# Attention over channels, then a gated feed-forward layer: q and k loaded eight rows at a time, and the first batch's norms by columns instead of by a row

## The chip, the core and the metric

The kernel runs on one core of one Trainium2 chip. The metric is the device time of one execution in microseconds (us). The engines are named as in the profile: PE (TensorE, matrix products), PEld (its weight loads), DVE (VectorE), ACT (ScalarE), POOL (GpSimd) and SP (SyncE). "DMA" is the 16 engines that move data between the main memory (HBM) and the core.

## The reference

There are four batches of q, k and v, each 6016 x 256, and weights of 256 x 1536 (gate and value) and 1536 x 256 (out). Attention runs between channels, not between tokens:

```python
qn = q / (np.linalg.norm(q, axis=1, keepdims=True) + 1e-06)   # norms over the tokens
kn = k / (np.linalg.norm(k, axis=1, keepdims=True) + 1e-06)
s = kn.transpose(0, 2, 1) @ qn / tau                           # 256 x 256 for each batch
a = np.exp(s - s.max(-1, keepdims=True))
a /= a.sum(-1, keepdims=True) + 1e-09
x = v @ a
gate = 1 / (1 + np.exp(-(x @ w_gate)))
out = (gate * (x @ w_val)) @ w_out
```

Inputs and output are float32; tau is 1.0 and known when the kernel is built.

## The kernel before

**Tiling.** A batch is read as 128 partitions x 47 rows of 256 channels; row t of a partition is one token. Rows go in chunks of four (TPC), twelve chunks to a batch, the last with three rows. DMAs from POOL's queue convert float32 to bf16 on the way. For each row the raw scores q^T k are added up in PSUM (`score`, two products of 128x256, tile ps_s), and the squares of q and k are added up for the norms. The scores are scaled by the inverse norms and exponentiated to e, of 256 x 256 in two halves.

**Folding.** Since x = v a, the kernel never forms x. It computes G = a w_gate and H = a w_val once for each batch (`gh`, 12 products of 2 matmuls each, in three groups of 512 columns, tiles ps_gh, gh_G, gh_H), with the division by the row sums (`sums`) at their eviction. Then, for each chunk of v, transposed (`transpose_v`, for the first two chunks on PE, later by DMA), `glu` makes for each of 12 blocks f the products ps_gate and ps_val (2 matmuls of 128x512 each), the sigmoid on ACT (g_sb) and the product on DVE (hT). `out_mms` multiplies hT by w_out for the chunk before (ps_o), and `flush` copies and stores.

**Order.** The order on every engine is written out by hand. All matmuls go through one helper, so they share the line L89 in the profile and are told apart by their tiles. While batch b is in the feed-forward loop, `side_work(b)` hangs loads, scores and norms of batch b + 1 onto the slots (chunk, f) of that loop. Only the first batch's attention has nothing to hide behind: it is written out ahead of the loop, and it is what the change is about.

**The first batch.** The first chunk of q and k comes over the SP and ACT queues in float32 and is converted by DVE and ACT. All others come over POOL's queue (`load_qk`, L98): ten pairs of transfers of four rows, then two rows and one row. Then follow, on the same queue, the first groups of w_gate and w_val (L144), the first chunk of v (L107), the other two groups of each, v's second chunk and w_out (L151). POOL's transfers share eight semaphores in turn, so each issue waits until the eighth transfer before it has landed. For each chunk DVE squares q and ACT squares k (L183, L181), DVE adds both to acc (L493), and PE makes the scores, followed by products that nobody reads (`busy`, tile ps_busy, five after each chunk), which keep it occupied while it waits for data. The last chunks' squares, and acc, are summed over partitions on PE into ps_n: for q as columns (`norm_q`, one column a product), for k as a row that stands in every partition (`norm_k`, 128x256 products).

**The tail ahead of the loop.** `roots` takes x^(1/2) as exp(ln(x)/2) on ACT (L301, L302), in two parts (q's columns with half of k's row, then the other half); both functions are in the same table as the exponential that follows. `weights` adds the epsilon and inverts on DVE (L273, L274, in `wide_inv`), scales the scores by q's and k's inverse norm in one DVE instruction for each half (L310), and exponentiates (L319). Eight `busy` products stand between. Then come the sums of e (L157, L158 invert them), four `gh` products, v's transposes between them (L400, evicted at L404 and L405), and two more `gh` products; ACT loads the Sigmoid table and the loop begins. Evictions of `gh` are at L383 (ACT) and L385 (DVE). The remaining six `gh` products stand in the loop's first slots:

```python
    gh(0, 4, pso, "o", act=False)
    gh(0, 5, pso, "o", act=False)
    ...
                if (b, ci) == (0, 0) and 0 < f <= len(gh_order) - 6:
                    gh(0, 5 + f, pso, "o")
```

Of the kernel before, what the change touches and what calls it, by code (L numbers as in the profile page):

```python
# [10 lines left out]
FP32 = mybir.dt.float32  # L11
BF16 = mybir.dt.bfloat16
ACT = mybir.ActivationFunctionType
# [5 lines left out]
def kernel(  # L19
# [47 lines left out]
    def pool(name, bufs, **kw):  # L67
        return ctx.enter_context(tc.tile_pool(name=name, bufs=bufs, **kw))

    consts = pool("consts", 1)  # L70
    qkpool = pool("qkpool", NCH)
    sqpool = pool("sqpool", 2)
# [20 lines left out]

    def load_qk(b, t0, nt):
        tiles = []
        for name, src in (("q", q), ("k", k)):
            tl = qkpool.tile([P, TPC, C], BF16, tag=name, name=name + "_sb")
            nc.gpsimd.dma_start(out=tl[:, :nt, :], in_=rows(src, b)[:, t0 : t0 + nt, :])  # L98
            tiles.append(tl)
        qk[b, t0] = tiles  # L100

# [9 lines left out]
    t0, nt = groups0[0]  # L111
    qk[0, 0] = [qkpool.tile([P, TPC, C], BF16, tag=n, name=n + "_sb") for n in ("q", "k")]
    first_f32 = [consts.tile([P, nt, C], FP32, name=f"first{w}") for w in range(2)]
    for eng, tl, src in zip((nc.sync, nc.scalar), first_f32, (q, k)):
        eng.dma_start(out=tl, in_=rows(src, 0)[:, t0 : t0 + nt, :])

    nc.scalar.add_instruction(
        mybir.InstLoadActFuncSet(
            name=nc.get_next_instruction_name(),
            engine=mybir.EngineType.Activation,  # L120
            act_func_set_id=list(get_activation_tables("trn2")).index("natural_log_exp_and_others"),
        )
    )
    load_qk(0, *groups0[1])

    ident_bf = consts.tile([P, P], BF16)
    make_identity(nc, ident_bf)
    ones_bf = consts.tile([P, P], BF16)
    nc.vector.memset(ones_bf, 1.0)
# [6 lines left out]
    nc.scalar.copy(qk[0, 0][1], first_f32[1])  # L136
    for t0, nt in groups0[2:]:
        load_qk(0, t0, nt)

    w_sb = [[consts.tile([P, CB, FG], BF16, name=f"w_{n}{fg}") for fg in range(NFG)] for n in ("gate", "val")]  # L140
    w_out_sb = consts.tile([P, FC, C], BF16)
    for fg in range(NFG):
        for w, src in enumerate((moe_w_gate, moe_w_val)):
            nc.gpsimd.dma_start(  # L144
                out=w_sb[w][fg],
                in_=src.rearrange("(t p) f -> p t f", p=P)[:, :, ds(fg * FG, FG)],
            )
        if fg == 0:
            load_v(0, 0)
    load_v(0, 1)  # L150
# [36 lines left out]

    def norm_q(ps, sq, nt, first, last):

        for u in range(nt):  # L190
            for j in range(CB):
                mm(
                    ps[:, j : j + 1],
                    sq[:, u, ds(j * P, P)],
                    ones_bf[:, 0:1],
                    start=(first and u == 0 and j == 0),
                    stop=(last and u == nt - 1),
                    skip_group_check=True,
                )

    def norm_k(ps, sq, nt, last, parts=1):

        n = C // parts
        for u in range(nt):
            for i in range(parts):
                mm(
                    ps[:, CB + i * n : CB + (i + 1) * n],
                    ones_bf,
                    sq[:, u, ds(i * n, n)],
                    start=False,  # L210
                    stop=(last and u == nt - 1),
                    skip_group_check=True,
                )

# [40 lines left out]
    def norms_mm(b):  # L255

        s = st[b]
        fold_q, fold_k = s["fold"]
        ps = psm.tile([P, CB + C], FP32, tag="m", name="ps_n")
        norm_q(ps, fold_q, 2, True, True)  # L260
        norm_k(ps, fold_k, 2, True)
        s["n"] = ps
# [29 lines left out]

    def roots(b, part):

        s = st[b]
        if part == 0:
            s["n_sb"] = attp.tile([P, CB + C], FP32, tag="nsb", name="n_sb")
            s["r"], s["rk"] = s["n_sb"][:, :CB], s["n_sb"][:, CB:]
        cols = slice(0 if part == 0 else CB + P, CB + (part + 1) * P)
        x = s["n_sb"][:, cols]  # L300
        nc.scalar.activation(out=x, in_=s["n"][:, cols], func=ACT.Ln)  # L301
        nc.scalar.activation(out=x, in_=x, func=ACT.Exp, scale=0.5)  # L302

    def weights(b, i):

        s = st[b]
        wide_inv(b, i)
        y = attp.tile([P, CB, P], FP32, tag=f"y{i}", name="y_sb")
        for j in range(CB):
            nc.vector.scalar_tensor_tensor(  # L310
                out=y[:, j, :],
                in0=s["s"][:, j, ds(i * P, P)],
                scalar=s["r"][:, j : j + 1],
                in1=s["rk"][:, ds(i * P, P)],
                op0=ALU.mult,
                op1=ALU.mult,
            )
        e = attp.tile([P, CB, P], BF16, tag=f"e{i}", name=f"e_sb{i}", bufs=2)
        nc.scalar.activation(out=e, in_=y, func=ACT.Exp, bias=shift)  # L319
        s.setdefault("e", []).append(e)  # L320
        s.setdefault("rrow", [])
# [42 lines left out]

    gh_order = [(0, w, i) for i in range(CB) for w in range(2)]
    gh_order += [(fg, w, i) for fg in range(1, NFG) for w in range(2) for i in range(CB)]

# [21 lines left out]

    def transpose_v(b, ci, ps=None):  # L390

        t0, nt = groups[ci]
        v_sb = vs.pop((b, ci))
        vT = vtpool.tile([P, TPC * CB, P], BF16, tag="vT", name="vT")
        flat = v_sb[:, :nt, :].rearrange("p t c -> p (t c)")
        if ps is None:
            nc.sync.dma_start_transpose(out=vT[:, : nt * CB, :], in_=flat)
        else:
            for n in range(nt * CB):
                nc.tensor.transpose(  # L400
                    out=ps[:, n, :], in_=flat[:, ds(n * P, P)], identity=ident_bf
                )
            half = nt * CB // 2
            nc.scalar.copy(vT[:, half : nt * CB, :], ps[:, half : nt * CB, :])  # L404
            nc.vector.tensor_copy(out=vT[:, :half, :], in_=ps[:, :half, :])  # L405
        vts[b, ci] = vT.rearrange("p (u cb) n -> p cb u n", cb=CB)

# [73 lines left out]
    busy(9)  # L481
    ps_n0 = psm.tile([P, CB + C], FP32, tag="m", name="ps_n")

# [4 lines left out]
    for g, (t0, nt) in enumerate(groups0):  # L488
        engines = (nc.vector, nc.scalar) if g < last0 else (nc.scalar, nc.vector)
        sq = [squares(0, t0, nt, w, engines[w], acc[w] if g == 0 else None) for w in range(2)]  # L490
        if 0 < g < n_acc:
            for w in range(2):
                nc.vector.tensor_tensor(out=acc[w], in0=acc[w], in1=sq[w], op=ALU.add)  # L493
        for u in range(nt):
            score(0, t0, u)
        if g < n_acc:
            busy(5)
        elif g == n_acc:
            norm_q(ps_n0, acc[0], TPC, True, False)
            norm_k(ps_n0, acc[1], TPC, False)  # L500
            norm_q(ps_n0, sq[0], nt, False, False)
            norm_k(ps_n0, sq[1], nt, False)
        elif nt == TPC:
            busy(2)
            norm_q(ps_n0, sq[0], nt, False, False)
            norm_k(ps_n0, sq[1], nt, False)
        elif g < last0:
            held = (sq, nt)
        else:
            (held_q, held_k), n = held  # L510
            norm_q(ps_n0, held_q, n, False, False)
            norm_k(ps_n0, held_k, n, False)
            norm_q(ps_n0, sq[0], nt, False, True)
            norm_k(ps_n0, sq[1], nt, True, CB)
    st[0]["n"] = ps_n0
    for i in range(CB):
        roots(0, i)
    busy(8)
    for i in range(CB):
        weights(0, i)  # L520
    gh_tiles(0)
    sums(0, 0)
    gh(0, 0, psg, "g", act=False)
    gh(0, 1, psv, "v", act=True)
    transpose_v(0, 0, psv.tile([P, TPC * CB, P], BF16, tag="v", name="ps_tp"))
    sums(0, 1, pss, "s")
# [3 lines left out]
    gh(0, 4, pso, "o", act=False)  # L530
    gh(0, 5, pso, "o", act=False)


    def side_work(b):
# [7 lines left out]
        for ci in range(NCH):  # L542
            nb, nci = (b, ci + 1) if ci + 1 < NCH else (b + 1, 0)
            lb, lci = (b, ci + 2) if ci + 2 < NCH else (b + 1, ci + 2 - NCH)
            if (nb, nci) == (0, 1):
                at(8, lambda: transpose_v(0, 1, psm.tile([P, TPC * CB, P], BF16, tag="m", name="ps_tp")))
            elif nb < B:
                at(ci * FC + 2, transpose_v, nb, nci)
# [6 lines left out]
        for g, (t0, nt) in enumerate(groups):  # L555
            s0 = first + g * (last - first) // NCH
            at(max(0, s0 - 20), load_qk, n, t0, nt)
            for u in range(nt):
# [25 lines left out]
    for b in range(B):  # L584
        side = side_work(b)
        for ci in range(NCH):
            block = b + 1 < B and ci in (9, 10)
            for f in range(FC):
# [4 lines left out]
                for fn, a in side.get((ci, f), ()):  # L593
                    fn(*a)
                if (b, ci) == (0, 0) and 0 < f <= len(gh_order) - 6:
                    gh(0, 5 + f, pso, "o")
# [46 lines left out]
```

## Time and profile before

| What | Value |
|---|---|
| median of 3 runs | 833.22 us (833.01 to 833.39) |
| profiled execution | 833.39 us, of which 831.3 us are the span of the profile |
| PE busy | 818.4 us, 98% of the span |
| DVE, ACT, POOL busy | 591.0, 390.6, 82.6 us |
| POOL's transfers (q0) | 38.81 MB written, 23920 packets |
| first gate product | at 43.38 us |
| PE idle before the first sums | 2.03 us, to 38.53 us |

The span is from the first to the last instruction of one execution. A time in the chain or the timeline counts from its start. In a row of the timeline the bracket says how long the engine had stood idle and what ended it. PE's busy time is modelled from the starts of its pipelined matmuls, so 98% busy says that it seldom waits, not that it computes at its peak. GB/s count bytes as they are written, so a load of float32 into bf16 reads twice that.

### The profile page before, as it was taken

What the parts mean: (1) busy time and instruction counts of PE and PEld (TensorE: products, weight loads), DVE (VectorE), ACT (ScalarE), POOL (GpSimd) and SP (SyncE); (2) the same over time, 40 slices, a digit from 0 to 9 for tenths busy, and PEclk for the clock granted to TensorE, in tenths of its full rate; (3) what the DMA queues carried; (4) which work ended last, traced back from release to release, by engine and by line L of the source; (5) the groups of instructions that cost most, each with busy time, mean ns of one, the idle gap of its engine ahead of it and who ended that gap; (6) DMA issues with size and microseconds to landing.
All of it is one profiled execution on the core that took longest, in us unless ns stands there. A gap on an engine that the chain in (4) does not pass through costs nothing.

```text
span 831.3 us, 13764 instructions
## 1 busy us (share of the span) xinstructions
PE 818.4 (98%) x5191; PEld 503.9 (61%) x5204; DVE 591.0 (71%) x1023; ACT 390.6 (47%) x644; POOL 82.6 (10%) x157
## 2 busy tenths in 40 slices
PE   7799999999999999999999999999999999999998
PEld 4546666666665666665566666666566566666666
DVE  6577787787667777778757777777766666666665
ACT  4464444446644444444654444444555444444442
POOL 5531100002111100000221010000000000000000
PEclk9999999999999999999999999999999999999999
DMA  9999522335947423322975353223322423322211
GB/s 210 206 206 208 108 52 54 83 64 109 173 84 133 95 58 84 61 52 60 180 140 103 85 118 64 51 48 89 64 48 61 86 52 79 74 49 65 50 35 71
DMA packets 79026, 77.17 MB, mean 93 GB/s; under 512 B 50800, under 2 KB 55920, under 8 KB 78960
## 3 DMA queue, kind: packets, MB, share of 16 engines
q0 software_dynamic: 23920, 38.81, 27.9%
q1 hardware_dynamic: 54752, 36.91, 17.5%
q8 instruction: 40, 0.66, 0.3%
q10 hardware_dynamic: 288, 0.59, 0.2%
q14 instruction: 26, 0.21, 0.1%
HBM read 78.64 MB, written 24.64 MB: 124 GB/s over the span
## 4 chain that ended last, share of the span: by engine, by line
PE 95%; DMA 3%; DVE 1%; issue 0%; ACT 0%; POOL 0%; DVEq 0%; POOLq 0%
PE ps_o L89 29%; PE ps_gate L89 29%; PE ps_val L89 29%; PE ps_s L89 4%; DMA k_sb<-in_k_dram 3%; PE ps_gh L89 3%; DVE hT L430 0%; PE ps_n L89 0%; DVE sq L183 0%; PE ps_end L89 0%; ACT g_sb L429 0%; PE ps_tp L400 0%; DVE n_sb L274 0%; POOL q_sb L98 0%; DVE n_sb L273 0%
## 5 line engine op out<-in xcount | busy, mean ns | idle before, releaser
L430 DVE TENSOR_TENSOR hT<-ps_val,g_sb 128x512 bf16<-128x512 f32 (+1 forms) x576 | 390.9, 679 | 205.1 <-ACT g_sb L429 199.9
L429 ACT ACTIVATE g_sb<-ps_gate 128x512 bf16<-128x512 f32 (+1 forms) x576 | 338.3, 588 | 385.9 <-PE ps_gate L89 379.1
L89 PE MATMUL ps_val<-vT,gh_H 128*128 128x512 bf16 (+1 forms) x1152 | 337.6, 375 | 0.3
L89 PE MATMUL ps_gate<-vT,gh_G 128*128 128x512 bf16 (+1 forms) x1152 | 337.5, 375 | 0.2
L89 PE MATMUL ps_o<-w_out_sb,hT 128*128 128x256 bf16 x2244 | 324.8, 273 | 0.0
L89 PEld LDWEIGHTS <-hT 128*128 128x128 bf16 x2268 | 221.0, 98 | 124.6
L89 PEld LDWEIGHTS <-gh_H 128*128 128x128 bf16 x1152 | 112.7, 98 | 131.7 <-issue 0.8
L89 PEld LDWEIGHTS <-gh_G 128*128 128x128 bf16 x1152 | 112.5, 98 | 37.4
L107 POOL DMA_DIRECT2D v_sb<-in_v_dram x48 | 25.5, 531 | 622.8 <-DMA vT<-v_sb 513.4
L456 DVE COPY out_sb<-ps_o 128x256 f32<-128x256 f32 x187 | 77.2, 413 | 12.6 <-PE ps_o L89 12.6
L89 PE MATMUL ps_s<-k_sb,q_sb 128*128 128x256 bf16 x376 | 66.0, 272 | 4.9 <-DMA k_sb<-in_k_dram 3.7
L89 PEld LDWEIGHTS <-q_sb 128*128 128x128 bf16 x376 | 36.7, 98 | 13.7 <-issue 6.3
L234 DVE TENSOR_TENSOR acc<-acc,sq 128x1024 bf16<-128x1024 bf16 (+1 forms) x66 | 44.1, 669 | 0.0
L183 DVE TENSOR_TENSOR sq<-q_sb 128x1024 bf16<-128x1024 bf16 (+2 forms) x44 | 29.3, 667 | 2.6 <-DMA q_sb<-in_q_dram 2.6
L98 POOL DMA_DIRECT2D k_sb<-in_k_dram x48 | 26.4, 550 | 17.7 <-DMA k_sb<-in_k_dram 7.9
L98 POOL DMA_DIRECT2D q_sb<-in_q_dram x48 | 26.2, 546 | 15.3 <-DMA q_sb<-in_q_dram 7.2
L183 DVE TENSOR_TENSOR sq<-k_sb 128x1024 bf16<-128x1024 bf16 (+2 forms) x34 | 22.4, 658 | 1.0 <-PE ps_n L89 1.0
L89 PE MATMUL ps_busy<-ones_wide,ones_bf 128*128 128x512 bf16 x61 | 17.3, 416 | 1.7 <-DVE shift L133 1.6
L181 ACT ACTIVATE sq<-k_sb 128x1024 bf16<-128x1024 bf16 (+1 forms) x11 | 11.2, 1018 | 14.5 <-DMA k_sb<-in_k_dram 11.7
L493 DVE TENSOR_TENSOR acc<-acc,sq 128x1024 bf16<-128x1024 bf16 x16 | 11.1, 691 | 5.5 <-ACT sq L181 5.3
L89 PEld LDWEIGHTS <-e_sb 128*128 128x128 bf16 x112 | 10.4, 101 | 7.6 <-ACT e_sb L319 2.7
L89 PE MATMUL ps_gh<-w_val,e_sb 128*128 128x512 bf16 x45 | 14.1, 390 | 0.4 <-issue 0.2
(61 smaller groups left out, 136.6 us busy)
## 6 DMA issues: line engine op xcount, KB each, us to landing
out_dram<-out_sb SPq DMA_DIRECT2D x44, 512.0 KB, 2.9
v_sb<-in_v_dram POOLq DMA_DIRECT2D x44, 256.0 KB, 3.8
q_sb<-in_q_dram POOLq DMA_DIRECT2D x43, 256.0 KB, 7.5
k_sb<-in_k_dram POOLq DMA_DIRECT2D x43, 256.0 KB, 8.6
out_dram<-out_sb SPq DMA_DIRECT2D x3, 384.0 KB, 2.5
w_gate<-in_moe_w_gate_dram POOLq DMA_DIRECT2D x3, 256.0 KB, 6.8
w_val<-in_moe_w_val_dram POOLq DMA_DIRECT2D x3, 256.0 KB, 7.4
w_out_sb<-in_moe_w_out_dram POOLq DMA_DIRECT2D x1, 768.0 KB, 12.6
```

What stands on the lines that cost most here:

```text
L89: nc.tensor.matmul(out, lhsT=lhsT, rhs=rhs, start=start, stop=stop, **kw)
L98: nc.gpsimd.dma_start(out=tl[:, :nt, :], in_=rows(src, b)[:, t0 : t0 + nt, :])
L107: nc.gpsimd.dma_start(out=v_sb[:, :nt, :], in_=rows(v, b)[:, t0 : t0 + nt, :])
L181: nc.scalar.activation(out=sq[:, :nt, :], in_=src[:, :nt, :], func=ACT.Square)
L183: engine.tensor_tensor(out=sq[:, :nt, :], in0=src[:, :nt, :], in1=src[:, :nt, :], op=ALU.mult)
L234: nc.vector.tensor_tensor(out=acc[:, :nt, :], in0=acc[:, :nt, :], in1=st[b]["sq", w][:, :nt, :], op=ALU.add)
L429: nc.scalar.activation(out=g_sb[:, :n], in_=ps_gate[:, :n], func=ACT.Sigmoid)
L430: nc.vector.tensor_tensor(out=hts[b, ci][:, f, :n], in0=ps_val[:, :n], in1=g_sb[:, :n], op=ALU.mult)
L456: nc.vector.tensor_copy(out=out_sb[:, s, :], in_=ps)
L493: nc.vector.tensor_tensor(out=acc[w], in0=acc[w], in1=sq[w], op=ALU.add)
```

## The change

- `load_qk` loads up to eight rows into a tile of eight rows, and gives its halves to the two chunks. The pool has 8 such tiles for q and for k instead of 12 of four rows. For the first batch that is four pairs of eight rows, then 4, 4, 2 and 1; for each later batch six pairs instead of twelve.
- On POOL's queue v's first chunk comes ahead of all weights. POOL also builds an identity in float32.
- The fillers become six after each chunk up to the last pair, one and two in that pair.
- All norms of the first batch, k's too, are summed as columns (ps_n is 128x4), rooted on ACT with Sqrt, and inverted on DVE. ACT then loads the table for Exp. k's inverse norms are spread into a row in every partition by a float32 product with the identity, one for each half (`spread_k`).
- DVE copies the scores to SBUF (`copy_s`), multiplies by the spread row (four times 128x128), and ACT exponentiates four times 128x128 with q's inverse norm as scale.
- Three fillers and one stand around the spreads instead of eight. v's transposes come ahead of the sums. Five instead of six `gh` products stand ahead of the loop, seven in it, and in the second and third group each half's G and H follow one another.

```diff
-    qkpool = pool("qkpool", NCH)
+    qkpool = pool("qkpool", 8)
...
-            tl = qkpool.tile([P, TPC, C], BF16, tag=name, name=name + "_sb")
+            tl = qkpool.tile([P, 2 * TPC, C], BF16, tag=name, name=name + "_sb")
             nc.gpsimd.dma_start(out=tl[:, :nt, :], in_=rows(src, b)[:, t0 : t0 + nt, :])
             tiles.append(tl)
-        qk[b, t0] = tiles
+        for u in range(0, nt, TPC):
+            qk[b, t0 + u] = [tl[:, u : u + TPC, :] for tl in tiles]
...
+    nc.scalar.preload_act_table(ACT.Sqrt)
+    pairs = [(t, 2 * TPC) for t in range(TPC, head - 3 * TPC, 2 * TPC)]
+    loads0 = pairs + [(t, n) for t, n in groups0 if t >= pairs[-1][0] + 2 * TPC]
+    load_qk(0, *loads0[0])
...
-    for t0, nt in groups0[2:]:
+    for t0, nt in loads0[1:]:
         load_qk(0, t0, nt)
+    load_v(0, 0)
...
-        if fg == 0:
-            load_v(0, 0)
...
+    def norms_sqrt(b):
+        s = st[b]
+        s["r"] = attp.tile([P, 2 * CB], FP32, tag="r", name="r")
+        nc.scalar.activation(out=s["r"], in_=s["n"], func=ACT.Sqrt)
+
+    def norms_inv(b):
+        r = st[b]["r"]
+        nc.vector.tensor_scalar(out=r, in0=r, scalar1=1e-6, scalar2=None, op0=ALU.add)
+        nc.vector.reciprocal(r, r)
...
+    def spread_k(b, i, pl, tag):
+
+        s = st[b]
+        ps = pl.tile([P, P], FP32, tag=tag, name="ps_rk")
+        mm(ps, s["r"][:, CB + i : CB + i + 1].to_broadcast([P, P]), ident_f, True, True)
+        s.setdefault("rk", []).append(ps)
...
+        nc.vector.tensor_copy(out=s["x"][:, j, :], in_=s["s"][:, j, :])
...
-        wide_inv(b, i)
-        y = attp.tile([P, CB, P], FP32, tag=f"y{i}", name="y_sb")
+        e = attp.tile([P, CB, P], BF16, tag=f"e{i}", name=f"e_sb{i}", bufs=2)
         for j in range(CB):
-            nc.vector.scalar_tensor_tensor(
-                out=y[:, j, :],
-                in0=s["s"][:, j, ds(i * P, P)],
-                scalar=s["r"][:, j : j + 1],
-                in1=s["rk"][:, ds(i * P, P)],
-                op0=ALU.mult,
-                op1=ALU.mult,
-            )
...
-        nc.scalar.activation(out=e, in_=y, func=ACT.Exp, bias=shift)
+            y = attp.tile([P, P], FP32, tag=f"y{i}{j}", name="y_sb")
+            nc.vector.tensor_tensor(
+                out=y, in0=s["x"][:, j, ds(i * P, P)], in1=s["rk"][i], op=ALU.mult
+            )
+            nc.scalar.activation(
+                out=e[:, j, :], in_=y, func=ACT.Exp, bias=shift, scale=s["r"][:, j : j + 1]
+            )
...
-    gh_order = [(0, w, i) for i in range(CB) for w in range(2)]
-    gh_order += [(fg, w, i) for fg in range(1, NFG) for w in range(2) for i in range(CB)]
+    gh_order = [(fg, w, i) for fg in range(NFG) for i in range(CB) for w in range(2)]
...
-            busy(5)
+            busy(6 if t0 < pairs[-1][0] else 1 if t0 == pairs[-1][0] else 2)
...
     st[0]["n"] = ps_n0
-    for i in range(CB):
-        roots(0, i)
-    busy(8)
-    for i in range(CB):
-        weights(0, i)
+    norms_sqrt(0)
+    nc.scalar.preload_act_table(ACT.Exp)
+    copy_s(0, 0)
+    norms_inv(0)
+    copy_s(0, 1)
+    busy(3)
+    spread_k(0, 0, pso, "o")
+    spread_k(0, 1, pso, "o")
+    busy(1)
+    weights(0, 0)
+    weights(0, 1)
+    late = []
+    transpose_v(
+        0, 0, psv.tile([P, TPC * CB, P], BF16, tag="v", name="ps_tp"), lambda *a: late.append(a)
+    )
+    nc.scalar.copy(*late.pop())
     gh_tiles(0)
     sums(0, 0)
     gh(0, 0, psg, "g", act=False)
     gh(0, 1, psv, "v", act=True)
-    transpose_v(0, 0, psv.tile([P, TPC * CB, P], BF16, tag="v", name="ps_tp"))
     sums(0, 1, pss, "s")
     gh(0, 2, psg, "g", act=False)
     gh(0, 3, psv, "v", act=True)
     nc.scalar.preload_act_table(ACT.Sigmoid)
     gh(0, 4, pso, "o", act=False)
-    gh(0, 5, pso, "o", act=False)
...
-                at(8, lambda: transpose_v(0, 1, psm.tile([P, TPC * CB, P], BF16, tag="m", name="ps_tp")))
+                at(7, lambda: transpose_v(0, 1, psm.tile([P, TPC * CB, P], BF16, tag="m", name="ps_tp")))
...
-            at(max(0, s0 - 20), load_qk, n, t0, nt)
+            if g % 2 == 0:
+                at(max(0, s0 - 20), load_qk, n, t0, min(2 * TPC, NT - t0))
...
-                if (b, ci) == (0, 0) and 0 < f <= len(gh_order) - 6:
+                if (b, ci) == (0, 0) and f < len(gh_order) - 5:
                     gh(0, 5 + f, pso, "o")
```

## The prediction

> **What bounds the kernel now.** I read the page first (engine shares, chain), then the chain of waits in order of time, then one-microsecond windows for the granted clock, and last the timeline of the first 45 us.
>
> ```profile
> span 831.3 us, 13764 instructions
> PE 95%; DMA 3%; DVE 1%; issue 0%; ACT 0%; POOL 0%; DVEq 0%; POOLq 0%
> ```
>
> TensorE (PE) ends 95% of the chain. The windows from 43.4 us to 800 us show it busy all the time but for some 0.05 us in a few stretches. Whatever removes idle time elsewhere than on PE is worth nothing there. What is left is the head: everything ahead of the first gate product. In the chain of waits (start, length, what) it reads:
>
> ```profile
> 20.88 10.61 DMA k_sb<-in_k_dram
> 31.53 1.03 PE ps_s L89 x8
> 34.29 0.49 PE ps_n L89 x10
> 34.81 0.29 ACT n_sb L301
> 35.12 0.32 ACT n_sb L302
> 35.46 0.76 DVE n_sb L273
> 36.24 0.98 DVE n_sb L274
> 37.32 0.62 DVE y_sb L310 x2
> 37.97 0.52 ACT e_sb L319
> 38.53 0.20 PE ps_r L89 x2
> 39.62 0.76 PE ps_tp L400 x8
> 41.17 2.37 PE ps_gh L89 x6
> 43.54 0.43 PE ps_gate L89 x2
> ```
>
> Up to 33.5 us the loads of q and k decide. Then 3.7 us go from the last norm product to the first weights e (34.78 to 38.53), and 4.9 us more to the first gate product: 43.38 us in the timeline. Columns of the next view are stretch, its length, busy us of PE, PEld, DVE, ACT, POOL, then the granted clock, DMA share and GB/s:
>
> ```profile
> 37.00:38.00 1.00, 0.00 (x0) 0.00 (x0) 0.89 (x4) 0.04 (x1) 0.12 (x1) 1.00 1.24 205
> 39.00:40.00 1.00, 1.00 (x10) 0.74 (x9) 0.89 (x5) 0.27 (x1) 0.53 (x1) 0.80 1.23 202
> 41.00:42.00 1.00, 0.82 (x2) 0.30 (x2) 0.65 (x3) 0.29 (x1) 0.30 (x1) 0.50 1.15 213
> 43.00:44.00 1.00, 1.00 (x6) 0.43 (x5) 0.87 (x2) 1.00 (x1) 0.51 (x1) 1.00 1.46 195
> ```
>
> PE stood idle for 2.03 us (36.5 to 38.53), and from about 39.6 to 43.0 us its clock was halved: there a 128x512 product takes 0.42 us instead of 0.215. So the old tail pays twice for its long wait. The weights and v come in the order of the POOL queue, and an issue waits for the eighth before it, so the issues tell the landings:
>
> ```profile
> 18.43 0.53 POOL L98 DMA_DIRECT2D k_sb<-in_k_dram  x1 [0.74 <-DMA k_sb<-in_k_dram]
> 19.66 0.53 POOL L98 DMA_DIRECT2D q_sb<-in_q_dram  x1 [0.70 <-DMA q_sb<-in_q_dram]
> 37.88 0.53 POOL L98 DMA_DIRECT2D q_sb<-in_q_dram  x1 [0.95 <-DMA v_sb<-in_v_dram]
> 39.12 0.53 POOL L98 DMA_DIRECT2D k_sb<-in_k_dram  x1 [0.70 <-DMA w_gate<-in_moe_w_gate_dram]
> ```
>
> One four-row transfer (524 KB read) lands each 1.23 to 1.25 us: 419 to 426 GB/s read, the queue always full. First gate weights landed by 35.1 us, first value weights by 36.37, v's first chunk at 37.88, second gate weights at 39.12.
>
> **The change, part by part.**
>
> *Loads.* 24 issues for the first batch become 16: four pairs of eight rows, then 4, 4, 2, 1. Bytes and their order on the path are the same, and the last transfers are as small as before, so the last k lands at the same 33.4 us if the rate holds. The trace has no eight-row transfer. Nearest rows: the four-row steps of 1.25 us in the middle and 1.5 us around 25 us. As bounds I take 1.23 and 1.35 us for each half of a new transfer; with 16 halves (about 20 us) that is -0.3 to +1.6 us. I take 0, the row nearest. [...] POOL builds one more identity (its two steps took 0.23 and 0.29 us for bf16) before its third issue, while 2 MB are queued: nothing.
>
> *Squares and adds.* They now start in pairs. DVE's three steps per chunk (0.69 each) need 2.07 of the 2.5 us in which a chunk lands. After the last pair (k at 26.55 us as now) DVE finishes at about 26.55 + 1.1 (ACT's square) + 4 x 0.69 = 30.4 us, then squares chunks 9 (31.05) and 10 (31.7). PE's norm products of chunk 9 end at about 31.75, so chunk 10's scores start 0.2 us later than today's 31.53. The 128x256 k-norm products (0.11 each) become twice as many of one column (about 0.045): 0.36 for 0.43 us a chunk. Together the last norm product ends at 34.9 us instead of 34.78. Bounds 34.4 (all caught up) and 35.3.
>
> *Norms to e.* ACT's root is 128x4: nearest row Ln 128x130, 0.28 us; I take 0.25 with hand-over (35.15). Then Exp's table: table loads in this trace take 1.28 us (36.45). Beside it DVE adds and inverts 128x4: 0.15 + 0.17 as for 128x1 (rows L157, L158) up to 0.74 + 0.97 as for 128x130; I take 0.35 (35.5). The two fp32 spreading products are not in the trace: from 0.076 us (a transpose: 8 in 0.61) to about 0.7; I take 0.4 each (36.35). Two scalings at 0.31 each after the first spread end at 36.55; two exponentials of 128x128, at 0.3 each (between 0.28 and 0.51), at 37.1 us. e's first half is there 1.4 us earlier than 38.5. Both copies of the scores (0.41, as L456) lie beside the root and the spreads.
>
> *PE afterwards.* Three fillers, the spreads, a filler and v's eight transposes (0.61; v now comes first and lands near 35.1) fill the wait to 37.2 us, so I expect no halved clock. Sums to 37.35, first gh product (0.43) to 37.8. The second needs the value weights, which are now third in the queue and land near 37.85: this wait is new but short. It ends at 38.3; second sums, products three to five to 39.7. DVE: half of vT 0.42 (37.7), reciprocal 0.35, eviction 0.75 (38.8), reciprocal 0.35, eviction 0.75: 39.9. First gate product at 39.95 us, 3.4 us before today's 43.38. ACT's second value eviction is done at 40.2, ahead of the value product at 40.4; the Sigmoid table (1.28) then ends at 41.5, ahead of the third gate product at 42.4.
>
> *Given back.* Five gh products stand ahead of the loop instead of six; the sixth costs 2 x 0.215 = 0.43 us inside it, where PE has no gap. The order of gh products after the first four changes nothing in count, and their weights (40.4 to 42.9 us) land before use.
>
> *Later batches.* Six pairs of transfers instead of twelve; today's are issued at 199 us for products after 239 us, and PE waits for none after 60 us. Eight tiles of eight rows hold more than twelve of four. For batch 1 the first two transfers (2 MB) should land near 54 us, ahead of the first score at about 57.8. If that cover went, it would cost what they are late: nothing at these numbers.
>
> Sum: -3.43 + 0.43 = -3.0 us. The profiled execution took 833.39 us (831.3 of span, 2.1 around it), the highest of the runs shown, 0.17 above their median of 833.22. So 830.4.
>
> **The rivals.**
>
> *The clock falls elsewhere.* With only one and two fillers in the last pair, and one-column products for norms, the stretch from 29.4 to 32.8 us has about 1.6 us of wide products. For it: 36.2 to 39.6 us of today had 1.4 us of PE work in 3.4 and was followed by the half clock. Against it: with the norm products counted PE is busy for 3 of the 3.4 us. At half clock six scores, two fillers and more cost about 1.2 us on the way to the root: first gate near 41.2, 831.6 us; with DVE held up as well (L273 took 0.74 us beside a POOL issue, 0.22 without) near 42, 832.5. [...]
>
> *The loads are slower.* If a transfer of eight rows moves its bytes more slowly, each per cent costs 0.2 us on some 20 us, plus what its coarser start costs. With everything else as forecast, 15% eats the 3.0 us, and from 24% the kernel is slower by over 1.67 us; at 30% it takes 836.4. For it: nothing in the trace shows such a transfer, and 23.4 to 28.1 us already lost 0.9 us with four rows. Against it: 208 to 211 GB/s written all along, descriptors only longer.
>
> *The gain is there but nothing waits for it.* If the value weights or DVE's evictions hold the first gate to 42 us or more, what remains is below 1 us: 832.5.
>
> **How the numbers follow.** Forecast 0.69 (its own range 829.0 to 831.5); clock or evictions 0.19 (831.6 to 833.2); slower loads 0.12 (to 836.4). The low end is a root at 34.4, quicker spreads and loads at 1.23 us: 829.0. The high end takes in the clock cases: 833.2. About 0.2%, 1.67 us, can be told from no change: faster means below 831.55. Faster 0.70, same 0.18, slower 0.12.
>
> **What would show it.** Right: k's last square near 33.7 us, a root of 128x4 near 34.9, first sums near 37.2, the first gate product near 40 us, clock 1.00 from 36 to 44 us, and no PE wait after 60 us. Wrong: last k landing later than 34.5, clock 0.50 rows between 30 and 43 us, PE waiting at the second gh product for w_val beyond 38.3, or waits for k_sb in later batches.

## The result and the profile after

The changed kernel takes 830.84 us (median of 6 runs, 830.13 to 831.14), the kernel before 833.25 us (median of 6 runs beside it, 832.65 to 833.39): ratio 0.9972 [0.9959, 0.9985], or 2.41 us less. The profiled executions are 833.39 and 830.87 us (spans 831.3 and 828.9), 2.52 us apart, and the traces account for all of it.

The page of the kernel after, the lines that answer to the first two shown of before:

```profile
span 828.9 us, 13710 instructions
PE 90%; DMA 7%; POOL 1%; DVE 1%; issue 0%; ACT 0%; POOLq 0%
```

PE's share of the chain fell from 95% to 90%, and DMA's rose from 3% to 7%. The chain of waits after (start, length, what) says which DMA that is:

```profile
...
36.20 12.60 DMA v_sb<-in_v_dram
48.81 22.32 DMA vT<-v_sb
71.18 0.60 PE ps_gate L88 x2
```

From 36 to 71 us the chain no longer runs through PE. It runs through v's third chunk: its load, then its transposition by DMA, then the gate product at 71.18 us that reads it.

The timeline of the kernel after (start, us, engine, line, operation, out<-in, form; in brackets the idle time before and who ended it). First the tail from the root to the first gate product, whose line numbers differ by one from before:

```profile
34.23 0.17 ACT L284 ACTIVATE r<-ps_n 128x4 f32<-128x4 f32 x1 [0.51 <-PE ps_n L88]
34.42 1.28 ACT L510 ACT_TABLE_LOAD   x1
34.97 0.68 PE L88 MATMUL ps_rk<-ident_f,r 128*128 128x128 f32 x4
35.46 0.88 DVE L314 TENSOR_TENSOR y_sb<-x_sb,ps_rk 128x128 f32<-128x128 f32 x4 [0.33 <-PE ps_rk L88]
35.78 1.65 ACT L317 ACTIVATE e_sb<-y_sb,shift,r 128x128 bf16<-128x128 f32 x4
36.72 0.18 PE L88 MATMUL ps_r<-ones_bf,e_sb 128*128 128x1 bf16 x1 [0.21 <-ACT e_sb L317]
38.98 0.73 PE L88 MATMUL ps_gate<-vT,gh_G 128*128 128x512 bf16 x2
```

The first sums of e now start at 36.33 and 36.72 us (38.53 before), and the first gate product at 38.98 us (43.38). The windows of the kernel after (stretch, its length, busy us of PE, PEld, DVE, ACT, POOL, granted clock, DMA share, GB/s) show full clock in this stretch, where before had 0.80 and 0.50:

```profile
37.00:38.00 1.00, 0.93 (x7) 0.50 (x7) 0.86 (x3) 1.00 (x4) 0.27 (x1) 1.00 1.25 208
39.00:40.00 1.00, 1.00 (x6) 0.33 (x5) 0.93 (x2) 0.98 (x2) 0.49 (x1) 1.00 1.23 199
41.00:42.00 1.00, 1.00 (x7) 0.47 (x5) 0.62 (x2) 0.93 (x3) 0.43 (x1) 1.00 1.11 196
```

The issues of eight-row transfers, from the timeline after:

```profile
18.11 0.53 POOL L98 DMA_DIRECT2D q_sb<-in_q_dram  x1 [1.93 <-DMA q_sb<-in_q_dram]
20.64 0.53 POOL L98 DMA_DIRECT2D k_sb<-in_k_dram  x1 [2.00 <-DMA k_sb<-in_k_dram]
```

They stand 2.53 us apart, so each half took 1.26 us, as the four-row transfers before did (1.23 to 1.25).

The last three lines, from the loop of the kernel after, have no counterpart before:

```profile
50.67 0.59 ACT L404 COPY vT<-ps_tp 128x512 bf16<-128x512 bf16 x1 [1.19 <-DVE vT L403]
51.81 0.59 PE L88 MATMUL ps_gate<-vT,gh_G 128*128 128x512 bf16 x2 [0.36 <-ACT g_sb L428]
71.18 0.60 PE L88 MATMUL ps_gate<-vT,gh_G 128*128 128x512 bf16 x2 [0.28 <-DMA vT<-v_sb]
```

At 50.67 us ACT had idled 1.19 us for DVE's copy of the other half of vT. Its sigmoid behind that came late, and two of PE's products came 0.52 and then 0.30 us behind PE's even step of 0.43 us. At 71.18 us PE waits for the DMA transposition; this product stands 0.44 us behind its place in the step. The brackets give less (0.36 and 0.28 us idle), because the ends of matmuls are modelled.

How far the kernel after is ahead, place by place, from the two timelines:

| place | before, us | after, us | ahead by, us |
|---|---|---|---|
| first gate product | 43.38 | 38.98 | 4.40 |
| first value product | 43.81 | 39.55 | 4.26 |
| less the sixth gh product, now inside the loop | | | 3.83 |
| first out product (ps_o), behind the waits at 51 and 52 us | 57.66 | 54.69 | 2.97 |
| a gate product behind the wait for vT at 71 us | 97.99 | 95.47 | 2.52 |
| ACT's table load at 418 us | 418.00 | 415.48 | 2.52 |
| profiled execution | 833.39 | 830.87 | 2.52 |

So the head brought 3.83 us net, and two places in the loop took back 1.3 us.

The profiled execution of before is one in which the clock fell, and not all are. Of the 62 executions of before that ran beside the experiments, 28 have a mean granted clock of 0.997 or 0.998 on record, as the profiled one has (0.998), and 34 have 0.999 or 1.000. Their medians are 833.24 and 832.79 us. So the half clock costs before about 0.45 us where it comes, and against its executions without it the change is worth about 1.95 us.

### The profile page after: what moved, and what is told of

It is laid out like the page before. It is cut to its first block, busy times and chain, and to the rows that moved or that the text cites. A ratio compares the mean times of both kernels' runs of the same rounds, so it can differ in the third digit from the quotient of the medians.

```text
span 828.9 us, 13710 instructions
## 1 busy us (share of the span) xinstructions
PE 815.9 (98%) x5204; PEld 502.9 (61%) x5218; DVE 588.2 (71%) x1023; ACT 391.0 (47%) x644; POOL 59.6 (7%) x115
## 4 chain that ended last, share of the span: by engine, by line
PE 90%; DMA 7%; POOL 1%; DVE 1%; issue 0%; ACT 0%; POOLq 0%
PE ps_o L88 29%; PE ps_gate L88 28%; PE ps_val L88 28%; PE ps_s L88 4%; DMA k_sb<-in_k_dram 3%; DMA vT<-v_sb 3%; PE ps_gh L88 2%; DMA v_sb<-in_v_dram 2%; DVE hT L429 0%; POOL w_val L145 0%; POOL w_gate L145 0%; DVE sq L182 0%; PE ps_end L88 0%; ACT g_sb L428 0%; POOL w_out_sb L150 0%
## 5 line engine op out<-in xcount | busy, mean ns | idle before, releaser
L182 DVE TENSOR_TENSOR sq<-k_sb 128x1024 bf16<-128x1024 bf16 (+2 forms) x34 | 22.4, 658 | 0.9 <-ACT sq L180 0.9
L382 ACT ACTIVATE gh_G<-ps_gh,rrow 128x512 bf16<-128x512 f32 x21 | 14.4, 687 | 12.7 <-PE ps_gh L88 8.8
L88 PE MATMUL ps_busy<-ones_wide,ones_bf 128*128 128x512 bf16 x57 | 16.1, 407 | 1.7 <-DVE shift L133 1.6
L384 DVE TENSOR_SCALAR gh_H<-ps_gh,rrow 128x512 bf16<-128x512 f32 x22 | 16.3, 743 | 1.6 <-PE ps_gh L88 1.6
L98 POOL DMA_DIRECT2D k_sb<-in_k_dram x26 | 14.2, 545 | 15.9 <-DMA k_sb<-in_k_dram 9.0
L98 POOL DMA_DIRECT2D q_sb<-in_q_dram x26 | 14.3, 550 | 13.3 <-DMA q_sb<-in_q_dram 7.2
```

Of the source, the lines that this page charges most:

```text
L88: nc.tensor.matmul(out, lhsT=lhsT, rhs=rhs, start=start, stop=stop, **kw)
L182: engine.tensor_tensor(out=sq[:, :nt, :], in0=src[:, :nt, :], in1=src[:, :nt, :], op=ALU.mult)
L382: nc.scalar.activation(out=dst, in_=ps, func=ACT.Copy, scale=r)
L384: nc.vector.tensor_scalar(out=dst, in0=ps, scalar1=r, scalar2=None, op0=ALU.mult)
```

## The experiments

Two theories for what the loop takes back. **Order:** the wait at 51 us comes from the order of the two copies in `transpose_v`, DVE's first. **Row size:** the transposition is slower because the transfers beside it now move eight rows. Their rivals: the slot in which the transposes stand (for the order), the time at which v's third chunk or the queue's order lets it start (for the row size), and that time won at one place only lengthens the next wait. For the head: is the gain the clock, the loads, the order of v, or the shorter way from norms to e?

**e1_order** (after, with ACT's copy issued ahead of DVE's in the loop):

```diff
             half = nt * CB // 2
+            if late is None:
+                nc.scalar.copy(vT[:, half : nt * CB, :], ps[:, half : nt * CB, :])
             nc.vector.tensor_copy(out=vT[:, :half, :], in_=ps[:, :half, :])
-            (nc.scalar.copy if late is None else late)(vT[:, half : nt * CB, :], ps[:, half : nt * CB, :])
+            if late is not None:
+                late(vT[:, half : nt * CB, :], ps[:, half : nt * CB, :])
```

> The changed kernel with one thing undone: the two copies that evict v's second transposed chunk are issued ACT first, DVE second, as before the change. Theory (budget): the changed kernel loses 0.52 + 0.30 us at 51.3 to 52.5 us because ACT's copy stands in its queue behind DVE's, which stands behind a product hT, so the next sigmoid and with it a gate product are late; with ACT first the wait ends, the lead over the kernel before at the end of the first chunk grows from 2.97 to about 3.8 us, and the time is about 830.0 us. Rival: the wait comes from the seven gh products with their evictions in the loop; then it stays, 830.8. A second rival: the lead is eaten by the wait for vT at 70.7 us, which ends when the DMA transpose lands (71.1 us) whatever PE does: then that wait grows by what is won here, and the total stays at 830.8.

830.81 us (8 runs), ratio to before 0.9975 [0.9965, 0.9985]: not faster than after. Windows from 50 to 54 us, first of after, then of this kernel:

```profile
50.00:54.00 4.00, 3.51 (x16) 1.45 (x15) 2.62 (x5) 2.57 (x5) 0.53 (x1) 1.00 1.08 215
```

```profile
50.00:54.00 4.00, 4.00 (x20) 1.85 (x19) 3.40 (x6) 2.99 (x6) 0.53 (x1) 1.00 1.05 210
```

PE's idle time there is gone, and the first ps_o stands at 53.92 us instead of 54.69. But from the timeline of e1_order:

```profile
71.04 0.60 PE L88 MATMUL ps_gate<-vT,gh_G 128*128 128x512 bf16 x2 [0.91 <-DMA vT<-v_sb]
```

The product at 71 us starts only 0.14 us earlier than in after. The order is the cause of the wait at 51 us, and the rival is right that this time is worth nothing while vT lands at 71 us.

**e2_slot** (after, the transposes of v's second chunk one slot later):

```diff
-                at(7, lambda: transpose_v(0, 1, psm.tile([P, TPC * CB, P], BF16, tag="m", name="ps_tp")))
+                at(8, lambda: transpose_v(0, 1, psm.tile([P, TPC * CB, P], BF16, tag="m", name="ps_tp")))
```

> The changed kernel with v's second chunk transposed in slot 8 again instead of slot 7. Theory (order of the copies): the wait near 52 us only moves by a slot, 0.8 us of PE idle stay. Rival (slot 7 collides with the last gh evictions): the wait falls to below 0.2 us.

830.86 us in one run. From first gate to first ps_o it takes 15.59 us against 15.71 in after and 14.90 in e1_order: the slot is worth 0.12 us, the order 0.81. The product at 71 us starts at 71.17. The theory holds, and the rival falls.

**e3_late4** (after, the eight-row tiles of later batches filled by two four-row transfers each; the first batch keeps eight):

```diff
+        step = 2 * TPC if b == 0 else TPC
...
+        for u in range(0, nt, step):
+            m = min(step, nt - u)
+            for tl, src in zip(tiles, (q, k)):
+                nc.gpsimd.dma_start(
+                    out=tl[:, u : u + m, :], in_=rows(src, b)[:, t0 + u : t0 + u + m, :]
+                )
```

> The changed kernel with the first batch's loads as they are (eight rows) and the later batches' tiles filled by two transfers of four rows each, in the order q, k, q, k. Theory (packets): the DMA transpose of v's third chunk shares each DMA engine packet by packet with POOL's transfers; with packets of 2 KB written instead of 4 KB it lands by 65 us, as before the change (64.2), the wait of 0.44 us at 70.7 us goes, 830.4 us. Rival (the transpose is late since v's third chunk or the queue's order is): it lands near 71 us again, 830.8.

830.37 us (6 runs), 0.9968 [0.9956, 0.998], 0.44 below e1_order in the same comparison. The transposition takes 16.1 us from issue to landing instead of 22.3, and the wait at 71 us is gone. Before the change it took 15.3. Its line in the DMA issues (last column: us to landing), of before and then of e3_late4:

```profile
vT<-v_sb SPq DMA_TRANSPOSE x1, 15.3
```

```profile
vT<-v_sb SPq DMA_TRANSPOSE x1, 16.1
```

It was issued at 48.95 us before and at 48.81 after, so the shorter head does not move it. The kernels with four or eight rows all bear the row size out: 22.1 to 22.5 us in the six with eight rows in later batches (after, e1, e2, e6, e7, e8), 15.2 to 16.1 us in the seven with four (before, e3, e4, e5, e9, e11, e12).

The wait at 51 us stays, and with it the first ps_o at 54.72. The DMA part of the profile shows how the row size does it: packets, MB and share of 16 engines in 4 us, before (56 to 60 us) and after (60 to 64 us). Queue q0 carries POOL's loads, q1 the transposition:

```profile
q0 software_dynamic: 391, 0.71, 93.9%
q1 hardware_dynamic: 391, 0.10, 18.0%
```

```profile
q0 software_dynamic: 197, 0.74, 95.3%
q1 hardware_dynamic: 196, 0.05, 11.4%
```

Both times the two queues get about the same number of packets, 391 to 391 and 197 to 196. With eight rows q0's packets are twice as large (0.74 MB / 197 = 3.8 KB against 1.8 KB), so the same bytes of q0 leave the transposition half as many packets. In each microsecond of these stretches it is one packet for one as well: 99 to 96, 92 to 95, 102 to 100 and 98 to 100 before, 49 to 50, 59 to 58, 40 to 39 and 49 to 49 after. These are counts over all 16 engines; the order on a single one is not shown.

**e4_both** (e1 and e3 together):

> The changed kernel with both: ACT's copy first, and later batches in transfers of four rows. Theory: both waits go, 830.84 - 0.86 - 0.44 = 829.5 us, 3.7 us faster than the kernel before. Rival (the waits are tied to one another or replaced by others): 830.2 or more.

829.48 us (5 runs, 829.33 to 829.78), 0.9958 [0.9946, 0.9971]: 3.4 us below before in the same comparison (832.87), 1.3 below e1_order and 0.9 below e3_late4. PE waits for nothing in the loop's first 30 us; windows of this kernel:

```profile
50.00:54.00 4.00, 4.00 (x23) 2.01 (x21) 3.28 (x6) 2.87 (x5) 1.70 (x4) 1.00 1.12 206
...
60.00:72.00 12.00, 12.00 (x78) 7.48 (x77) 8.47 (x15) 5.07 (x9) 4.78 (x9) 1.00 1.12 198
```

The row size pays by itself (e3). The order of the copies pays only where the later wait has been taken out. This version beats both kernels.

**e10_late2** (e4_both with later batches in two-row transfers):

```diff
-        step = 2 * TPC if b == 0 else TPC
+        step = 2 * TPC if b == 0 else TPC // 2
```

> The changed kernel with ACT's copy first, and the later batches' tiles filled by transfers of two rows each, so packets of 1 KB written. Theory (the DMA transpose shares each engine packet by packet, and what it waits for is the size of the other queue's packet): from 22.3 us with eight rows and 16.1 with four, the transpose of v's third chunk lands in 11 to 13 us, and nothing waits: 829.5 us, since four rows were early enough. Rival (only the number of transfers ahead of it counts): about 16 us.

829.47 us in one run: no gain, since nothing waits any more. But the transposition's line in the DMA issues of e10_late2:

```profile
vT<-v_sb SPq DMA_TRANSPOSE x1, 9.7
```

It came out even shorter than expected, and 9.7 us can't be put down to the row size alone. From 51 to 52 us both queues of e10_late2 move as in the other kernels:

```profile
q0 software_dynamic: 180, 0.16, 104.7%
q1 hardware_dynamic: 191, 0.05, 23.3%
```

Again nearly as many packets on both, of 0.9 KB on q0, and 191 in one microsecond for the transposition, against 98 beside four rows and 49 beside eight (391 and 196 in 4 us above). But from 52 to 58 us all queues together moved only 97 GB/s, where before had 205 and after 200 in the stretches above, and the transposition got 863 packets against 401 of q0. What held q0 back there is not shown. The rival falls without this run: with eight rows fewer transfers stand ahead of the transposition than with four, and it takes longer.

**e5_warm** (before, with 17 fillers instead of 8 in the tail, to hold the clock up):

```diff
-    busy(8)
+    busy(17)
```

> The kernel before with 17 instead of 8 unread products in the tail, so that PE does not idle from 36.5 to 38.5 us. Theory: the half clock from 39.6 to 43.0 us goes, the first gate product comes at about 42.3 instead of 43.38 us, 832.1 us. This is the share of the gain that is due to the clock. Rival (the evictions on DVE decide the first gate product, not the clock): less than 0.3 us, 833.0.

832.80 us (10 runs), 0.9998 [0.9989, 1.0008]. The clock stays at 1.00, and the first gate product comes at 42.18 us, 1.20 earlier. Then, from its timeline:

```profile
42.94 0.39 PE L89 MATMUL ps_gate<-vT,gh_G 128*128 128x512 bf16 x1 [0.39 <-DVE gh_G L385]
```

Its second half waits for DVE's eviction, and the first ps_o is only 0.48 us ahead of before's. So the half clock cost before at most half a microsecond; its evictions would have bound it anyway. The rival is nearer, and the executions on record say the same: none of these ten has the fall (mean clock 1.000), and their median is that of before's executions without it (832.80 in this comparison).

**e6_load8** (before with only the loads and fillers of the change: eight-row tiles and pairs, `busy(6 ... 1 ... 2)`, six pairs in later batches):

```diff
-    load_qk(0, *groups0[1])
+    pairs = [(t, 2 * TPC) for t in range(TPC, head - 3 * TPC, 2 * TPC)]
+    loads0 = pairs + [(t, n) for t, n in groups0 if t >= pairs[-1][0] + 2 * TPC]
+    load_qk(0, *loads0[0])
...
-            busy(5)
+            busy(6 if t0 < pairs[-1][0] else 1 if t0 == pairs[-1][0] else 2)
```

> The kernel before with the loads in eight-row transfers and the fillers as in the change, its tail as it was. Theory: the loads alone bring nothing: last k lands within 0.3 us of before, the first gate product within 0.5 us of 43.4, 833.2 us; vT of the third chunk lands near 71 us but is needed only at 73.9, so no wait. Rival (eight-row loads carry the gain): the first norms' root comes 0.5 us earlier or more, 832.5 or less.

832.48 us (10 runs), 0.9994 [0.9984, 1.0003]: 0.58 us less by the medians, which the interval does not tell from nothing. The time is the rival's, but not for its reason: the root starts at 34.90 us (34.81 before), and the first sums come at 38.42 us (38.53 before). All ten executions have a mean clock of 1.000, so part of the 0.58 is the fall that they don't have; against before's executions without it 0.3 us is left. The transposition takes 22.4 us here too, and nobody waits, since this kernel needs it later, at about 73 us. In its profiled execution PE idled 1.84 us ahead of the sums, and the clock did not fall (1.00 in the windows from 36 to 44 us).

**e11_vfirst** (before, with v ahead of the weights and its transposes ahead of the sums, as in the change):

```diff
+    load_v(0, 0)
...
-        if fg == 0:
-            load_v(0, 0)
...
+    transpose_v(0, 0, psv.tile([P, TPC * CB, P], BF16, tag="v", name="ps_tp"))
     gh_tiles(0)
```

> The kernel before with v's first chunk ahead of the weights in POOL's queue and its transposes ahead of the first sums on PE, and nothing else. Theory: the transposes (0.61 us) fall into PE's idle time, the first gate product comes 0.5 to 0.9 us earlier, but DVE takes v's copy between the scalings and the first eviction, which gives 0.4 of it back: 832.3 to 832.8 us. So most of the gain is left to the shorter way from the norms to e (sums at 36.7 instead of 38.5 us). Rival (the order of v and the transposes is the gain): 831.8 or less.

833.53 us (10 runs), 1.0004 [0.9995, 1.0013]: no gain, against both expectations. The sums stand at 38.27 us as e is no earlier, the clock falls from 40.5 to 44 us (0.50 in the windows), and the first gate product comes at 43.47. DVE's copy of vT lies at 40.48 to 40.90 us and the second value product of gh starts behind it. The clock fell in six of the ten; the other four have a median of 833.3 us, still no gain. Order alone brings nothing. Taken with e5 and e6, this leaves the shorter way from norms to e as what moves the sums from 38.5 to 36.7 us. The trace of e9_head4 below shows it directly: that kernel has the new tail on loads and fillers as before the change, with v first as here. Its sums stand at 36.51 and 36.90 us, 2.1 and 2.5 us behind its root at 34.41. Here they stand 3.7 us behind the first root (34.55). Which part of the new tail brings how much was not run.

**e7_vlater** (after, with the first gate and value weights ahead of v in POOL's queue, as before):

```diff
-    load_v(0, 0)
...
+        if fg == 0:
+            load_v(0, 0)
```

> The changed kernel with POOL's queue as before: first gate weights, first value weights, then v's first chunk. Theory: v lands near 37.7 us instead of about 35.1, and its transposes stand ahead of the first sums on PE, so these wait from 36.3 to about 37.8: the first gate product moves from 39.0 to about 40.4 us, and PE idles for 2 us, after which a stretch with half the clock may follow; 832.0 to 832.5 us. Rival (DVE's evictions decide anyway): 831.2 or less.

831.57 us (10 runs), 0.9984 [0.9974, 0.9993]: 0.73 us more than after. PE waits for v's first chunk until 36.95 us, the first ps_o is 1.0 us later (55.70), and vT is not waited for. So with the new tail the order of v matters, though on the old one it did not. It cost less than expected, because v in third place had landed by 36.95 us. Reading landings from POOL's issues had put the third place near 37.85, in another kernel. In this trace POOL's issue that waited for the same landing starts at 37.47 us, 0.5 us after PE could use v: such an issue gives only the latest time of a landing.

**e8_fill5** (after, with five fillers behind every chunk):

```diff
-            busy(6 if t0 < pairs[-1][0] else 1 if t0 == pairs[-1][0] else 2)
+            busy(5)
```

> The changed kernel with five fillers after every chunk, the last pair included (the change has one and two there). Theory: seven products of 0.215 us more after the last pair put PE behind the data by about 1 us at chunk 9, and the DVE-bound norm products of chunk 9 let it catch up only in part: the root comes 0.3 to 1.0 us later, 831.2 to 831.8 us. Rival (PE has slack there): 830.8. A second rival (fewer fillers had cost clock): faster than 830.8; the clock rows of the changed kernel, 1.00 throughout, speak against it.

830.86 us (10 runs, 830.65 to 831.37), 0.9975 [0.9966, 0.9985]. In the profiled execution, the slowest of the ten, the root starts 0.74 us later and the first ps_o 0.75 us later (55.44). The product at 71 us then starts at 71.48 us without a wait, only 0.30 later than after's. The median is the same as after's: the time is the rival's (830.8), though the root moved as the theory said. Where vT bounds, most of what fewer fillers bring to the head is not seen.

**e9_head4** (e4_both with four-row transfers and five fillers in the first batch as well):

```diff
-        step = 2 * TPC if b == 0 else TPC
+        step = TPC
...
-            busy(6 if t0 < pairs[-1][0] else 1 if t0 == pairs[-1][0] else 2)
+            busy(5)
```

> The changed kernel with ACT's copy first, and with all loads of q and k, the first batch's too, in transfers of four rows, with five fillers after each chunk as before the change. Against the same kernel with eight-row transfers in the first batch (829.48 us). Theory (the loads bring nothing; the gain is the tail's): last k lands within 0.2 us, DVE is not behind by a pair any more, the root comes at 33.9 to 34.5 us, 829.2 to 829.8 us. Rival (eight-row transfers with few fillers after the last pair carry part of the gain, as the 0.75 us by which the root moved with five fillers might say): 830.0 to 830.3 us.

830.17 us (6 runs, 829.88 to 831.72), 0.997 [0.9958, 0.9981], and no wait in the loop. The two longest (831.38 and 831.72) have a mean clock of 0.998, so the clock fell there too; the other four have a median of 829.97, 0.5 us behind e4_both's 829.48. That lies between theory and rival. In the profiled executions the first ps_o is at 54.06 us, 0.55 behind e4_both's 53.51, but e4_both has the earliest root of all executions with its head (33.86; the others 33.99 to 34.26, here 34.41). So eight-row loads with fewer fillers for the last pair do bring some 0.5 us, once nothing later absorbs it. How it divides was not run; e8, with the fillers alone undone, had its root 0.74 us later in its longest execution, which points to the fillers.

**e12_nofill** (e4_both without the fillers of the last pair, of the chunk of rows 40 to 43 and of the tail):

```diff
-            busy(6 if t0 < pairs[-1][0] else 1 if t0 == pairs[-1][0] else 2)
+            if t0 < pairs[-1][0]:
+                busy(6)
...
-            busy(2)
...
-    busy(3)
...
-    busy(1)
```

> The changed kernel with ACT's copy first and later batches in four-row transfers (829.48 us), here without the fillers of the last pair, of the chunk of rows 40 to 43 and of the tail. Theory (fillers are only there for the clock): the root comes up to 0.2 us earlier; if a stretch of 3.4 us with little PE work is followed by half the clock, rows of 0.50 appear after 33 us and the time is 830.0 to 831.0 us. Rival (norm products, spreads and transposes keep the clock): 829.2 to 829.5 us.

The four runs gave 832.24, 829.68, 829.21 and 829.05 us (0.9955 [0.994, 0.997]). The profiled one is the first; its windows:

```profile
31.00:34.00 3.00, 3.00 (x41) 2.32 (x38) 1.00 (x3) 2.04 (x3) 2.56 (x4) 0.56 1.24 205
...
39.00:41.00 2.00, 2.00 (x8) 0.79 (x7) 1.31 (x4) 0.79 (x2) 0.83 (x2) 0.50 1.23 209
```

The clock fell twice, the first gate product came at 41.82 us (38.61 in e4_both), and the execution took 2.8 us more than e4_both. The other three have a mean clock of 1.000 on record (0.996 in the profiled one), so there it did not fall, and their times lie about the rival's. Without a fall the fillers bring nothing: these three are no slower than e4_both. With the change's fillers none of 37 executions (after, e1 to e4, e7, e10) shows a fall. That they insure against it is likely, but one fall in four is little to go by.

## Why the prediction was right, point by point

It said 830.4 us from a head 3.43 us shorter and 0.43 us given back; 830.84 was measured. The direction and the mechanism in the head held. That the size is so close is in part luck: two terms were off by more than the result is, and they nearly cancel, about 1 us too little for the head and 1.3 us of waits in the loop that were not foreseen.

- **Loads: right.** The value taken was no change in rate, and the eight-row steps were 2.53 us for two halves, 1.26 each against 1.23 to 1.25 before: in a queue kept full, fewer and larger transfers gained nothing. e6 gives 0.9994 [0.9984, 1.0003] for the loads and fillers alone.
- **Squares, adds, norms: about 0.7 us too late.** The last k's square came at 33.46 us (said: 33.73), the scores of chunk 10 at 31.39 (said: 31.75), the root at 34.23 (said: 34.9). This is the mis-sized term of the head: 0.27 us lie ahead of the last square, and 0.40 behind it, where the one-column norm products made the way to the root 0.77 us long (1.17 said, 1.08 before). Between executions of the same head the root scatters by 0.4 us (34.23, 34.26, 33.99, 34.26, 33.86 and 34.11 in after, e1, e2, e3, e4 and e10).
- **Norms to e: the sum held, its pieces did not.** Add and inverse took 0.17 + 0.18 (said 0.35). The spreads took 0.68 for four products (said 0.8 for two; the 0.7 us that bounded this estimate from above stands in no row of before, and each spread took 0.34), the scalings 0.88 for four (said 0.31 each), the exponentials 1.65 for four, 0.41 each, instead of 0.3. Root to sums was 2.49 us (said 2.3).
- **PE afterwards: right in DVE's chain.** From the root to the end of the second eviction it was forecast 5.0 us, and it took 5.03 (34.23 to 39.26). But the first gate product's first half does not need that eviction, and started 0.3 us before it; its second half waited, at 39.32. With 0.67 from the root this makes the 0.97 us between 39.95 and 38.98. The short wait for the value weights did not happen: the second gh product came at 37.20 us right behind the first. Its landing had been read from POOL's issues, which come late: in after, the issue that waits for these weights starts at 37.73 us, 0.5 us after PE used them.
- **The half clock: worth less than the reading of before says.** "So the old tail pays twice" holds for some executions only, and there for about 0.45 us at the end (e5, and the 62 executions above). The tail's row L273 of 0.22 us, if that is what the first rival sets against 0.74 us "beside a POOL issue", also had a POOL issue beside it (37.88 us), so POOL is not shown to be the reason.
- **Given back: right.** The sixth gh product cost its 0.43 us.
- **Later batches: wrong.** "If that cover went ... nothing at these numbers" asked when the scores need q and k, and those did come in time. The step did not ask who shares the DMA engines with the longer transfers. The transposition of v's third chunk did: 22.3 us instead of 15.3. It put the product at 71 us 0.44 us behind PE's step in after and 1.07 in e1 (0.28 and 0.91 us idle by the brackets), and in e3 the wait is gone. "No PE wait after 60 us" is wrong for this reason.
- **The copies' order: not costed at all.** The change also turns the two copies of `transpose_v` round, in lines that its list and the diff shown leave out (e1 turns them back): DVE's copy of the first half of vT is now issued ahead of ACT's of the second, and in the loop ACT's next instruction is a sigmoid that PE needs. It cost 0.8 us (e1: 14.90 against 15.71 us from gate to ps_o).

The rivals. *Clock falls elsewhere*: it did not, with the fillers that the change has; in e12's profiled execution, without them, it did, at about the price forecast (first gate 41.82, said near 41.2 to 42). *Loads slower*: no. *The gain is there but nothing waits for it*: for the first gate this was wrong, but it happened 30 us later and at another waiter. After, e1 and e2, whose first ps_o spread from 53.92 to 54.69 us, all start the product at 71 us between 71.04 and 71.18, and all take 830.8 to 830.9 us.

What stays open: the division of e9's 0.5 us between loads and fillers, what held the loads back in e10, and why e8's median equals after's, though its profiled execution is 0.5 us longer.

## What to carry to other kernels

Where a change makes transfers longer on one queue, look for another queue that must land something beside them, and ask what share it keeps; a transfer's size was here a cost to its neighbour (22.3 us instead of 15.3 for the transposition), though it cost its own queue nothing. After a head is shortened, follow the chain to the next thing that does not move with it (here a DMA landing at 71 us): below that point further gains in the head were invisible until it was moved too (830.8 to 830.9 us in after, e1 and e2, 829.48 in e4). The order of two evictions on two engines should follow which engine is waited for next (0.81 us from gate to ps_o here).

## What the runs showed of the hardware

- Beside a full queue of loads the DMA transposition got about one packet for each of theirs: 196 to 197 beside rows of eight (after) and 391 to 391 beside four (before) in 4 us, 191 to 180 beside two (e10) in 1 us. That is 49, 98 and 191 packets in a microsecond, beside packets of 3.8, 1.8 and 0.9 KB. From issue to landing it took 22.1 to 22.5 us beside eight and 15.2 to 16.1 beside four.
- The same program runs with and without a fall of the clock. 2.03 us of idle PE was followed by the half clock in before's trace, yet 34 of 62 executions of before have no fall on record; in e6, with 1.84 us of idle PE in its trace, none of ten has one. The four half-clock stretches in the traces are all 3.4 us long (before 39.6 to 43.0 us, e11 40.5 to 43.9, e12 31.4 to 34.8 and 38.2 to 41.6), and e12's two start 6.8 us apart, twice that length. What decides whether an execution has the fall is not shown by any run here.
